# A gated mix of linear attention and a squared-ReLU layer on one Trainium2 core: the planner that lists all engines' work gets other durations and two tables of offsets, and copies may go to either of two engines

## The chip, the core and the metric

One of the eight cores of a Trainium2 chip runs the program alone. The metric is the device time of one execution in microseconds (us), the median of several. Five instruction queues run side by side and meet through semaphores: TensorE (PE, with its weight loads shown apart as PEld), VectorE (DVE), ScalarE (ACT), GpSimd (POOL) and SyncE (SP, which here only issues DMAs). Each queue takes its instructions in the order in which the program lists them.

## The reference

The input `x` is 2048 x 448. One branch is linear attention with 16 heads of 28, the other a feed-forward layer with 1792 hidden units. A sigmoid gate per row mixes them. Cut to what is computed:

```python
q, k, v = split(x @ wqkv)                      # 16 heads of 28
phi = lambda t: where(t > 0, t + 1, exp(t)) + 1e-6
kv  = einsum("bhsd,bhse->bhde", phi(k), v)     # one 28x28 matrix per head
den = einsum("bhqd,bhd->bhq", phi(q), phi(k).sum(seq)) + 1e-6
a   = (einsum("bhqd,bhde->bhqe", phi(q), kv) / den) @ wo
h   = relu(x @ w1 + b1) ** 2
b   = h @ w2 + b2
g   = sigmoid((x * gate_w).sum(-1))
out = g * a + (1 - g) * b
```

## The kernel before, in words

**Numbers as pairs.** Every float32 operand of a product is written as two parts of type float32r: a rounded "hi" copy and the rest, "lo = value - hi". A product is then three matmuls (hi hi, hi lo, lo hi). So whatever goes into TensorE first needs a copy (`split_hi`) and a subtraction (`split_lo`). `split_hi` is told its engine, mostly ACT; `split_lo` runs on DVE, for some operands on POOL.

**Two halves of the array.** A contraction of 128 rows is cut into the lower 64 rows (`LO`) and the upper 64 (`UP`). A matmul uses one half of TensorE's rows, so two matmuls run at once, one on each half; the text calls the halves lanes. All matmuls of one result accumulate in one PSUM bank, first those of one lane, then those of the other. Both lanes have the same amount to do.

**The stages.** Tokens are cut into 4 blocks of 512 and 16 tiles of 128. `h_ps{b}_{f}` is x @ w1 for block b and hidden tile f (14 of them, 21 matmuls of 512 columns each); `hidden` evicts it: ReLU on ACT, square on ACT, hi copy on DVE, lo on DVE. `o_ps{b}_{0 or 7}_{i}` is h @ w2 for 128 tokens over seven hidden tiles (matmuls of 448 columns). In the first half of the program, to about 220 us, f runs over 0 to 6 for all blocks; beside it run the keys `k_ps{t}` (450 columns), the Gram sums x'phi(k) `g_ps{b}_{c}`, then the key sums `z_ps`, `kv_ps` and `m_ps` (kv times wo). In the second half f runs over 7 to 13 for the blocks 3, 0, 1, 2, beside the queries `q_ps{b}_{c}`, the denominators `d_ps{b}`, and the attention outputs `a_ps{t}`. From a `d_ps` to the first `a_ps` of its block DVE has a long row of work: the addition of 1e-6, four reciprocals, four multiplications, and a hi and lo part for each of four tiles `q`.

**Eight PSUM banks.** Four (`acc_p`) hold `o_ps`, two (`mm_p`) `h_ps`, two (`ms_p`) everything else. A bank is used again when its last reader is done. In the first block `h_ps0_0` and `h_ps0_1` lie in `mm_p`, `h_ps0_2` and `h_ps0_3` in `ms_p`.

**What sets the order.** Nothing runs when it is written. The class `Flow` records the operations of ACT, DVE, POOL and SP (`queue`, L205), each with a cost from `cost` (L219), and the products as jobs in steps (L1000 and on). Then `run` (L375) plays the program through: again and again it asks each queue for the operation that could start first (`candidate`, L235) and each lane for the product that could start first (`product`, L329, looking `AHEAD` = 12 jobs on), takes the earliest, and writes its instruction into the program at that place. Among operations that could start at the same time the lower rank goes first; the rank is the moment when an operation was recorded plus `patience`. The constants of L32 to L35 say how long a matmul keeps its lane (`C512`, `C448`), how long after a matmul's end a reader can start (`LATE`), how long a semaphore takes (`SIGNAL`), a DMA (`LANDING`), and the change of a bank from lane to lane (`HANDED`). The numbers are only used to choose the order: on the chip each queue runs in that order and waits on semaphores.

## Time and profile before

| what | value |
|---|---|
| median of 3 runs | 440.94 us (440.69 to 441.06) |
| the profiled execution | 441.48 us, its span 439.7 us |
| granted TensorE clock | 1.000 |
| busy, of 439.7 us | PE 433.8, PEld 413.3, DVE 268.5, ACT 172.2, POOL 67.5 us |
| DMA | 29.02 MB, mean 66 GB/s |

The span runs from the first to the last instruction of the profiled execution; its own time is 1.8 us longer. A busy PE is not PE at its peak: a record of a 64-row matmul of 512 columns is 394 ns long, and two lanes with such records overlap, so that PE reads as busy when only one lane works. How fast PE goes is therefore read from how many matmuls start in a stretch.

### The profile page before, as it was taken

To read this page: it belongs to the slowest core of one execution; us is meant where nothing else is said; L and a number is where in the kernel's file an instruction comes from. 1 tells how busy PE (TensorE), PEld (TensorE's weight loads), DVE (VectorE), ACT (ScalarE), POOL (GpSimd) and SP (SyncE) were. 2 spreads that over 40 slices of the span, in tenths; PEclk is the share of its full clock that TensorE was granted. 3 is DMA by queue.
4 is the path that set the end of the run, shared out by engine and by line. 5 is a ranking of instruction groups with operands and counts; after the bars stand their busy time and mean duration, and the time that the engine had idled before them with its cause. 6 is when DMAs were issued, how large, how long until landed. Compare 5 with 4: busy or idle time off the path is not lost.

```text
span 439.7 us, 9349 instructions
## 1 busy us (share of the span) xinstructions
PE 433.8 (99%) x3978; PEld 413.3 (94%) x3978; DVE 268.5 (61%) x454; ACT 172.2 (39%) x298; POOL 67.5 (15%) x91
## 2 busy tenths in 40 slices
PE   8999999999999999999999999999999999999996
PEld 6899999999999999989999999999999899998995
DVE  4798525753587416783555849949535983458624
ACT  5846324532254214561533526415324242322530
POOL 0134104510065002530004900000000000000000
PEclk9999999999999999999999999999999999999999
DMA  7652210040111302223124631011210210001002
GB/s 255 240 152 87 76 46 25 23 138 25 41 59 45 113 3 66 83 84 92 41 86 112 110 92 49 0 64 34 62 49 1 85 25 1 0 33 55 1 1 83
DMA packets 17994, 29.02 MB, mean 66 GB/s; under 512 B 2544, under 2 KB 12448, under 8 KB 17952
## 3 DMA queue, kind: packets, MB, share of 16 engines
q1 hardware_dynamic: 16544, 26.81, 19.6%
q0 software_dynamic: 1408, 1.61, 2.2%
q8 instruction: 31, 0.51, 0.5%
q14 instruction: 11, 0.09, 0.1%
HBM read 22.08 MB, written 3.67 MB: 59 GB/s over the span
## 4 chain that ended last, share of the span: by engine, by line
PE 91%; DVE 5%; ACT 1%; DMA 1%; issue 0%; SPq 0%; DVEq 0%; ACTq 0%
PE h_ps L310 31%; PE o_ps L310 28%; PE a_ps L310 8%; PE g_ps L310 8%; PE k_ps L310 7%; PE q_ps L310 7%; DVE slot L209 4%; ACT slot L209 1%; PE kv_ps L310 1%; DMA slot<-in_xt 1%; DVE q L209 1%; PE m_ps L310 1%; PE d_ps L310 0%; ACT x L209 0%; PE z_ps L310 0%
## 5 line engine op out<-in xcount | busy, mean ns | idle before, releaser
L310 PE MATMUL h_ps<-x,w 64*128 64x512 f32 x1176 | 257.3, 394 | 0.4 <-ACT x L209 0.3
L310 PE MATMUL o_ps<-w_all,slot 64*128 64x448 f32 (+1 forms) x1332 | 240.5, 363 | 0.4 <-DVE slot L209 0.4
L310 PEld LDWEIGHTS o_ps<-w_all,slot 64*128 64x128 f32 (+1 forms) x1332 | 205.7, 184 | 6.5 <-DVE slot L209 1.8
L310 PEld LDWEIGHTS h_ps<-x,w 64*128 64x128 f32 x1176 | 193.6, 185 | 7.5 <-ACT x L209 0.8
L209 ACT ACTIVATE slot<-h_ps,few 128x512 f32<-128x512 f32 x56 | 38.0, 686 | 95.8 <-PE h_ps L310 83.8
L310 PE MATMUL q_ps<-x,wq_s 64*128 64x512 f32 x308 | 74.3, 393 | 0.0
L310 PE MATMUL k_ps<-wkm,x 64*128 64x450 f32 x336 | 66.3, 364 | 0.0
L209 DVE TENSOR_TENSOR slot<-slot,slot 128x512 fp32r<-128x512 f32 (+2 forms) x85 | 61.3, 733 | 4.4 <-DMA slot<-slot 1.7
L310 PE MATMUL a_ps<-wkm,q 64*128 64x448 f32 x336 | 62.2, 361 | 0.1
L310 PEld LDWEIGHTS k_ps<-wkm,x 64*128 64x128 f32 x336 | 57.0, 185 | 1.4 <-ACT slot L209 0.2
L310 PEld LDWEIGHTS q_ps<-x,wq_s 64*128 64x128 f32 x308 | 55.1, 184 | 1.5 <-DVE slot L209 0.3
L310 PEld LDWEIGHTS a_ps<-wkm,q 64*128 64x128 f32 x336 | 53.8, 184 | 1.3 <-DVE slot L209 0.6
L310 PE MATMUL g_ps<-p,nh 64*128 64x448 f32 x256 | 54.5, 359 | 0.0
L209 ACT ACTIVATE slot<-slot 128x512 f32<-128x512 f32 (+2 forms) x69 | 42.4, 625 | 14.7 <-DVE slot L209 13.8
L209 DVE CAST slot<-slot 128x512 fp32r<-128x512 f32 (+1 forms) x58 | 24.9, 430 | 31.9 <-ACT slot L209 30.7
L310 PEld LDWEIGHTS g_ps<-p,nh 64*128 64x128 f32 x256 | 40.6, 184 | 0.5
L209 POOL TENSOR_TENSOR nl<-slot,nh 128x384 fp32r<-128x384 f32 x16 | 19.3, 1209 | 117.6 <-ACT nh L209 117.6
L310 PE MATMUL g_ps<-p,nl 64*128 64x448 f32 x96 | 32.0, 360 | 0.0
L209 DVE SCALAR_TENSOR_TENSOR part<-part,gate,slot 128x448 f32<-128x448 f32 x13 | 8.8, 683 | 31.2 <-ACT slot L209 31.2
L209 ACT ACTIVATE slot<-a_ps,gate 128x448 f32<-128x448 f32 x16 | 10.0, 634 | 42.7 <-PE a_ps L310 40.7
L209 POOL TENSOR_TENSOR ksum<-ksum,slot 128x448 f32<-128x448 f32 x15 | 19.7, 1314 | 27.6 <-DVE slot L209 23.0
L209 DVE SCALAR_TENSOR_TENSOR slot<-slot,slot 128x448 f32<-128x448 f32 (+1 forms) x32 | 22.0, 688 | 1.7 <-ACT slot L209 1.5
(69 smaller groups left out, 350.0 us busy)
## 6 DMA issues: line engine op xcount, KB each, us to landing
slot<-in_xt SPq DMA_DIRECT2D x27, 256.0 KB, 2.8
slot<-in_xn SPq DMA_DIRECT2D x16, 224.0 KB, 2.5
out<-slot SPq DMA_DIRECT2D x16, 224.0 KB, 1.9
slot<-in_w SPq DMA_DIRECT2D x14, 224.0 KB, 2.8
slot<-in_w1a SPq DMA_DIRECT2D x8, 256.0 KB, 2.8
slot<-in_w1b SPq DMA_DIRECT2D x8, 192.0 KB, 4.0
wkm<-m POOLq DMA_DIRECT2D x24, 56.0 KB, 2.4
slot<-in_wq SPq DMA_DIRECT2D x4, 256.0 KB, 2.6
```

The costliest lines, as they stand in the source:

```text
L209: op = Op(lambda: method(*[real(x) for x in args], **{k: real(x) for k, x in kwargs.items()}), self.cost(name, kind, out, [x for x in aps ...
L310: ins = pe.matmul(b.ps[where or b.whole], real(a), real(m), start=b.seen == 1 + j.whole, stop=b.seen == b.total)
```

## The change

The reference, the products, their number and their operands stay as they are. What changes:

- **The planner's numbers.** Durations of matmuls, engine operations, signals and DMAs get other values. `cost` knows more forms (a scale per row, a read from PSUM). An engine is free again a little before an operation's end (`OVERLAP`), since the next one starts before the last is written.
- **Either engine.** A new helper `copy(to, src)` records a copy in the queues of both ACT and DVE (`either`), and the planner gives it to the engine where it would end first. `split_hi` always uses it, whatever engine its caller names; so do the copies of the first Gram sums and of `q_ps{b}_3`.
- **Two tables.** `SHIFT` adds to the rank of all operations that were recorded when a bank was done or a step entered (values from -16.5 to 33 us). `MOVE` adds to the place of a bank's job in the list of jobs (-4 to 3.5 steps), which sorts the products anew.
- **Two banks.** `h_ps0_2` and `h_ps0_3` lie in `acc_p` instead of `ms_p`.
- **Smaller things.** The key sums wait for all keys' banks in the plan, and the first tile to be done starts the sum on POOL, as the tiles now come in another order.

```diff
-C512, C448 = 0.2305, 0.204
+C512, C450, C448 = 0.2325, 0.2055, 0.2025
 AHEAD, PATIENCE, SPARE = 12, 5.0, 3
-LATE, SIGNAL, LANDING, HANDED = 0.25, 0.08, 1.9, 0.4
+LATE, SIGNAL, TO_PE, LANDING, HANDED = 0.17, 0.035, 0.09, 1.4, 0.22
+OVERLAP = {"act": 0.1, "dve": 0.085, "pool": 0.05, "sp": 0.0}
...
+SHIFT = {"a_ps0": -1.5, "a_ps1": -6, "a_ps10": 9, "a_ps11": -3, "a_ps13": -6, "a_ps14": -4.5, "a_ps15": -3, "a_ps4": 6,
...
+MOVE = {"a_ps0": 1.5, "a_ps11": 0.5, "a_ps12": 1.5, "a_ps13": 1, "a_ps14": 3.5, "a_ps15": -1.5, "a_ps2": -1.5, "a_ps3":
...
-    def __init__(self, emit, cost, after, rank, takes=None, size=0):
-        self.emit, self.cost, self.after, self.rank = emit, cost, after, rank
+
+    def __init__(self, ways, after, rank, takes=None, size=0):
+        self.ways, self.after, self.rank = ways, after, rank
         self.takes, self.size, self.end = takes, size, None
+        self.least = min((cost for _, cost in ways.values()), default=0.0)
...
+    def either(self, **calls):
+
+        self.queue({name: (getattr(unit, method), method, args, kwargs)
+                    for name, (unit, method, args, kwargs) in calls.items()})
...
-    def queue(self, name, method, kind, args, kwargs):
+    def queue(self, calls):
+        (name, (_, kind, args, kwargs)), *_ = calls.items()
         aps = [x for x in (*args, *kwargs.values()) if isinstance(x, View) or hasattr(x, "tensor")]
         out = kwargs.get("out", args[0] if args else None)
-        parts = [(x, x is out) for x in aps]
-        op = Op(lambda: method(*[real(x) for x in args], **{k: real(x) for k, x in kwargs.items()}),
-                self.cost(name, kind, out, [x for x in aps if x is not out], args),
-                {o for x, writes in parts for o in self.meeting(x, writes)}, self.now + self.patience,
+        n = next(k for k, x in enumerate(aps) if x is out)
+        ins = aps[:n] + aps[n + 1:]
+
+        def way(name, method, kind, args, kwargs):
+            return (lambda: method(*[real(x) for x in args], **{k: real(x) for k, x in kwargs.items()}),
+                    self.cost(name, kind, out, ins, args))
+        op = Op({n: way(n, *call) for n, call in calls.items()},
+                {o for x in aps for o in self.meeting(x, x is out)},
+                self.now + self.patience + SHIFT.get(self.label, 0.0),
                 out.hold if isinstance(out, View) else None, free_size(out) * list(like(out).ap)[0][1] * 4
                 if kind == "dma_start" else 0)
-        for x, writes in parts:
-            self.note(x, op, writes)
-        self.queues[name].append(op)
+        for x in aps:
+            self.note(x, op, x is out)
+        for n in calls:
+            self.queues[n].append(op)
...
+        scaled = any(free_size(x) == 1 for x in ins)
         if kind == "dma_start":
-            return 0.54 if name == "pool" else 0.06
+            return 0.51 if name == "pool" else 0.45
         if name == "act":
             f = args[2] if len(args) > 2 else None
-            return {AF.Relu: 0.26, AF.Exp: 0.18}.get(f, 0.25 if ps and f else 0.205) + n * 0.000835
+            base = 0.26 if f == AF.Relu or ps and scaled else 0.17 if ps else 0.295 if scaled else 0.2
+            return base + n * 0.000835
         if name == "pool":
-            return 0.25 + n * 0.002 if wide > 1 else 0.4 + n * 0.001
+            return 0.25 + n * 0.0021 if wide > 1 else 0.4 + n * 0.001
         if kind == "reciprocal":
-            return 0.13 + n * 0.006
+            return 0.13 + n * 0.0063
         if kind == "memset":
             return 0.1
-        return 0.155 + n / 960 if wide > 1 or ps else 0.1 + n * 0.00064
+        return 0.06 * scaled + (0.155 + n / 960 if wide > 1 or ps else 0.093 + n * 0.00064)
...
-            key = (max(start, self.free[name] + 0.05), op.rank)
+            more = op.ways[name][1] - op.least
+            key = (max(start, self.free[name] + 0.05) + more, op.rank)
             if best is None or key < best[0]:
-                best = key, start, k
-        return best and best[1:]
+                best = key, start + more, k, start
+        return best
...
-        op = self.queues[name].pop(k)
+        op = self.queues[name][k]
+        for n in op.ways:
+            self.queues[n].remove(op)
+        emit, cost = op.ways[name]
         if op.takes is not None and op.takes.buffer is None:
             place = self.vacant(op.takes.kind)[1]
             place[1], op.takes.buffer = op.takes, place[0](op.takes.dt) if callable(place[0]) else place[0]
-        self.tc.keep_in_program_order(op.emit())
-        self.free[name] = op.end = start + op.cost
+        self.tc.keep_in_program_order(emit())
+        op.end = start + cost
+        self.free[name] = op.end - OVERLAP[name]
         if op.size:
-            self.dma = max(self.dma, start + 0.6) + op.size / 385e3
+            self.dma = max(self.dma, start + 0.6) + op.size / 260e3
...
-            j.ready[s] = max([op.end + SIGNAL for op in wrote], default=0.0)
+            j.ready[s] = max([op.end + TO_PE for op in wrote], default=0.0)
...
+            self.label = b.name
             b.done()
...
-        self.jobs = [[(n, j) for n, step in enumerate(steps)
-                      for j in step.jobs[step.turn * s:] + step.jobs[:step.turn * s]] for s in range(2)]
+        self.jobs = [sorted([(n, j) for n, step in enumerate(steps)
+                             for j in step.jobs[step.turn * s:] + step.jobs[:step.turn * s]],
+                            key=lambda x: x[0] + MOVE.get(x[1].bank.name, 0.0)) for s in range(2)]
...
+    def copy(to, src):
+        flow.either(act=(nc.scalar, "activation", (to, src, AF.Copy), {}), dve=(nc.vector, "tensor_copy", (to, src), {}))
+
     def split_hi(eng, hi, src):
-        if eng is act:
-            act.activation(hi, src, AF.Copy)
-        elif eng is pool:
-            pool.tensor_scalar(hi, src, 1.0, 0.0, op0=ALU.mult, op1=ALU.add)
-        else:
-            eng.tensor_copy(hi, src)
+        copy(hi, src)
...
-        return [Job(bank, lambda: key_terms(t), C448, [("x", t // 4, False), "wk"])]
+        return [Job(bank, lambda: key_terms(t), C450, [("x", t // 4, False), "wk"])]
...
-        if t == 0:
+        if not pend:
...
-                act.copy(gsum[c], bank.ps[:, :D])
+                copy(gsum[c], bank.ps[:, :D])
...
-        return [Job(bank, key_sums, 0.07, ["zk"], [key_banks[NT - 1]])]
+        return [Job(bank, key_sums, 0.112, ["zk"], list(key_banks.values()))]
...
-        return [Job(kv_bank, kv_terms, 0.19, ["wv"], [grams[NB - 1, c] for c in range(4)])]
+        return [Job(kv_bank, kv_terms, 0.0985, ["wv"], [grams[NB - 1, c] for c in range(4)])]
...
-            act.copy(v, ps)
+            copy(v, ps)
...
-    first = [up_bank(0, f, *((mm_p, "mm") if f < 2 else (ms_p, "ms"))) for f in range(4)]
+    first = [up_bank(0, f, *((mm_p, "mm") if f < 2 else (acc_p, "acc"))) for f in range(4)]
```

In the new program ACT has 91 fewer of these copies and DVE 91 more. The program's order on each engine follows for three places. A row is one instruction, or several alike in a row (x2); in a bank's name come block, tile and half, the last number is a running one.

**TensorE, at the end of the first four `h_ps` banks.** Before, the last rows of `h_ps0_1` and what follows:

```order
L310 MATMUL h_ps0_1_210<-x0_76,w10_80 128x512
L310 MATMUL k_ps0_351<-wkm_83,x0_76 128x450 x2
L310 MATMUL k_ps0_351<-wkm_83,x1_77 128x450
L310 MATMUL k_ps0_351<-wkm_83,x0_76 128x450 x2
L310 MATMUL k_ps0_351<-wkm_83,x1_77 128x450
L310 MATMUL k_ps0_351<-wkm_83,x0_76 128x450 x2
L310 MATMUL k_ps0_351<-wkm_83,x1_77 128x450
L310 MATMUL k_ps0_351<-wkm_83,x0_76 128x450
L310 MATMUL k_ps0_351<-wkm_83,x1_77 128x450
L310 MATMUL k_ps1_376<-wkm_83,x0_76 128x450
L310 MATMUL k_ps0_351<-wkm_83,x0_76 128x450
L310 MATMUL k_ps1_376<-wkm_83,x0_76 128x450
```

After, a little later than that place (`k_ps2` has begun four rows behind the last `h_ps0_1`):

```order
L369 MATMUL k_ps0_353<-wkm_83,x1_77 128x450
L369 MATMUL k_ps2_361<-wkm_83,x0_76 128x450
L369 MATMUL o_ps0_0_0_388<-w2_all_82,slot11_365 128x448
L369 MATMUL k_ps2_361<-wkm_83,x1_77 128x450
L369 MATMUL o_ps0_0_0_388<-w2_all_82,slot11_365 128x448
L369 MATMUL k_ps2_361<-wkm_83,x1_77 128x450
L369 MATMUL o_ps0_0_0_388<-w2_all_82,slot12_375 128x448
L369 MATMUL k_ps0_353<-wkm_83,x0_76 128x450
L369 MATMUL o_ps0_0_1_400<-w2_all_82,slot11_365 128x448
L369 MATMUL k_ps0_353<-wkm_83,x0_76 128x450
```

Before, `k_ps0` stands alone over its first eleven matmuls, all in the lower lane, and the next rows of the upper lane are `k_ps0` again. Now `k_ps2` fills the upper lane beside `k_ps0`, and `o_ps0_0_0`, which reads the split `h` (slot11 is hi, slot12 lo), stands right behind them.

**VectorE, behind the denominators of block 3.** Before, the end of the row of work from `d_ps3` (which begins with two additions, four reciprocals and a read of `q_ps0_0`) up to the read that frees the bank of `q_ps0_1`, where `a_ps12` is to go:

```order
L209 TENSOR_TENSOR slot3_3660<-slot1_3849,slot3_3660 128x512
L209 TENSOR_TENSOR slot0_3739<-slot1_3849,slot0_3739 128x512
L209 TENSOR_TENSOR slot9_3583<-slot1_3849,slot9_3583 128x512
L209 TENSOR_TENSOR q2_3254<-slot8_3425,q0_3252 128x512
L209 TENSOR_TENSOR q4_3256<-slot3_3660,q1_3253 128x512
L209 TENSOR_TENSOR q6_3258<-slot0_3739,q3_3255 128x512
L209 SCALAR_TENSOR_TENSOR q7_3259<-slot9_3583,few_73,q5_3257 128x512
L209 SCALAR_TENSOR_TENSOR slot4_3857<-slot4_3857,slot10_3910 128x512
L209 TENSOR_TENSOR q5_3257<-slot9_3583,q7_3259 128x512
L209 SCALAR_TENSOR_TENSOR slot14_3842<-slot4_3857,few_73,slot14_3842 128x512
L209 CAST slot8_4004<-slot2_3890 128x512
L209 TENSOR_SCALAR slot3_4011<-q_ps0_1_3879 128x512
```

After, the same stretch; ahead of it stand two additions, four reciprocals, a hidden tile's split, four operations of block 0's `q_ps0_3`, two multiplications and the cast of q0. The bank of `q_ps0_0` takes `a_ps15`, that of `q_ps0_1` takes `a_ps13`:

```order
L258 CAST q1_3264<-slot9_3678 128x512
L258 TENSOR_TENSOR q2_3265<-slot4_3371,q0_3263 128x512
L258 TENSOR_TENSOR q3_3266<-slot9_3678,q1_3264 128x512
L258 TENSOR_TENSOR slot11_3666<-slot10_3780,slot11_3666 128x512
L258 TENSOR_TENSOR slot13_3562<-slot10_3780,slot13_3562 128x512
L258 CAST slot8_3939<-slot6_3863 128x512
L258 TENSOR_TENSOR q6_3269<-slot11_3666,q4_3267 128x512
L258 SCALAR_TENSOR_TENSOR q7_3270<-slot13_3562,few_73,q5_3268 128x512
L258 TENSOR_TENSOR slot2_3960<-slot6_3863,slot8_3939 128x512
L258 TENSOR_TENSOR q5_3268<-slot13_3562,q7_3270 128x512
L258 TENSOR_SCALAR slot9_3977<-q_ps0_0_3787 128x512
L258 TENSOR_SCALAR slot10_3986<-q_ps0_1_3900 128x512
```

The hi parts of q0 and q1 are now DVE's casts; before, all four were ACT's. From the additions to the read that frees the bank of the first `a_ps` DVE has 20 instructions before and 26 now. On TensorE 111 rows lie between the last of `d_ps3` and the first of these `a_ps` before, 142 now.

**TensorE, near the end.** Before, the first read of the split of `h_ps2_12` (slot3 is its hi part), 31 rows behind that bank's last matmul:

```order
L310 MATMUL a_ps11_5969<-wkm_83,q13_3265 128x448
L310 MATMUL a_ps11_5969<-wkm_83,q11_3263 128x448 x2
L310 MATMUL a_ps11_5969<-wkm_83,q7_3259 128x448
L310 MATMUL a_ps11_5969<-wkm_83,q2_3254 128x448
L310 MATMUL a_ps11_5969<-wkm_83,q8_3260 128x448
L310 MATMUL o_ps2_7_1_5614<-w2_all_82,slot12_5801 128x448
L310 MATMUL o_ps2_7_2_5618<-w2_all_82,slot3_5984 128x448
L310 MATMUL o_ps2_7_1_5614<-w2_all_82,slot12_5801 128x448
L310 MATMUL o_ps2_7_2_5618<-w2_all_82,slot3_5984 128x448
```

After, the first read of it (slot11):

```order
L369 MATMUL a_ps11_5966<-wkm_83,q0_3263 128x448
L369 MATMUL o_ps2_7_3_5666<-w2_all_82,slot6_5840 128x448
L369 MATMUL a_ps11_5966<-wkm_83,q10_3273 128x448
L369 MATMUL o_ps2_7_0_5639<-w2_all_82,slot11_5774 128x448
L369 MATMUL a_ps11_5966<-wkm_83,q13_3276 128x448
L369 MATMUL o_ps2_7_0_5639<-w2_all_82,slot11_5774 128x448
L369 MATMUL a_ps10_5939<-wkm_83,q9_3272 128x448
L369 MATMUL o_ps2_7_0_5639<-w2_all_82,slot12_5788 128x448
L369 MATMUL a_ps10_5939<-wkm_83,q9_3272 128x448
```

It now stands 181 rows behind the bank's last matmul: both last hidden banks, `h_ps2_12` and `h_ps2_13`, are done 150 rows and more before the program's end, and the attention tiles `a_ps8` to `a_ps11` stand behind them.

More of the change, by code (lines that the diff above doesn't have):

```diff
@@ L132, in __init__ @@
         self.tiles, self.queues, self.free, self.holds, self.kept, self.readers, self.shapes = {}, {}, {}, {}, {}, {}, {}
-        self.now, self.patience, self.dma, self.switched = 0.0, 0.0, 1.3, -1.0
+        self.label, self.now, self.patience, self.dma, self.switched = None, 0.0, 0.0, 0.0, -1.0
     def buffers(self, kind, tiles, like=None):
@@ L352, in enter @@
             if self.steps[self.entered - 1].before:
+                self.label = f"step{self.entered - 1}"
                 self.steps[self.entered - 1].before()
@@ L403, in run @@
             if event[1] == 0:
-                self.dispatch(event[3], event[4], event[0])
+                self.dispatch(*event[3:])
             else:
-                self.start(event[2], event[3], event[0])
+                self.start(event[2][0], event[3], event[0])
         if any(self.queues.values()) or any(self.at[s] < len(self.jobs[s]) for s in range(2)):
```

11 lines of the change are left out of this document (6 added, 5 removed), and 31 rows, old and new, of tables (MOVE, SHIFT).

## The prediction

> **What bounds the kernel now.** I read the page's busy times and its shares of the chain that ended last, then the groups by form for the count of matmuls, then the chain itself for TensorE's pace and for the places where it leaves TensorE.
>
> ```profile
> PE 433.8 (99%) x3978; PEld 413.3 (94%) x3978; DVE 268.5 (61%) x454; ACT 172.2 (39%) x298; POOL 67.5 (15%) x91
> PE 91%; DVE 5%; ACT 1%; DMA 1%; issue 0%; SPq 0%; DVEq 0%; ACTq 0%
> ```
>
> TensorE carries 91% of the chain, DVE 5% and ACT 1%. As no matmul is taken away, only waits can go. How much waiting is there? The counts:
>
> ```profile
> L310 PE MATMUL h_ps<-x,w 64*128 64x512 f32 x1176 | 257.3, 394 | 0.4 <-ACT x L209 0.3
> L310 PE MATMUL o_ps<-w_all,slot 64*128 64x448 f32 x1320 | 237.8, 362 | 0.4 <-DVE slot L209 0.4
> L310 PE MATMUL q_ps<-x,wq_s 64*128 64x512 f32 x308 | 74.3, 393 | 0.0
> L310 PE MATMUL k_ps<-wkm,x 64*128 64x450 f32 x336 | 66.3, 364 | 0.0
> L310 PE MATMUL a_ps<-wkm,q 64*128 64x448 f32 x336 | 62.2, 361 | 0.1
> L310 PE MATMUL g_ps<-p,nh 64*128 64x448 f32 x256 | 54.5, 359 | 0.0
> L310 PE MATMUL g_ps<-p,nl 64*128 64x448 f32 x96 | 32.0, 360 | 0.0
> ```
>
> The pace, from pieces of the chain without a wait (start, length, what), and its last pieces:
>
> ```profile
> 68.67 1.22 PE k_ps L310 x12
> 285.05 1.80 PE a_ps L310 x18
> 287.30 2.33 PE h_ps L310 x20
> ...
> 431.62 4.47 PE o_ps L310 x28
> 436.12 0.68 DVE slot L209
> ```
>
> With both lanes at work a 512-column matmul starts every 2.33/20 = 0.1165 us, one of 448 columns every 0.100, one of 450 every 0.102. So 1484 x 0.1165 + 2008 x 0.100 + 336 x 0.102 = 172.9 + 200.8 + 34.3 = 408.0 us. The small groups (`d`, `m`, `z`, `kv` and the last 12 full-height matmuls), counted in the code at these paces, I put at 11 us: 419 us of work. The first product starts at 5.38 us (row below) and the last ends at 431.62 + 4.47 = 436.09: 430.7 us. TensorE therefore loses some 12 us. A change of the order can win from these 12 alone; the 5.4 us ahead of them and the 3.6 us behind (the last bank's read, 0.68 us, and its store) stay.
>
> Where they are lost, at the start (timeline, all engines and weight loads):
>
> ```profile
> 5.38 8.85 PE L310 MATMUL h_ps<-x,w 64*128 64x512 f32 x68 [0.30 <-ACT x L209]
> 15.84 1.26 ACT L209 ACTIVATE slot<-h_ps,few 128x512 f32<-128x512 f32 x2 [1.43 <-PE h_ps L310]
> 16.58 2.37 PEld L310 LDWEIGHTS k_ps<-wkm,x 64*128 64x128 f32 x12 [0.25 <-ACT slot L209]
> 19.14 1.95 PEld L310 LDWEIGHTS k_ps<-wkm,x 64*128 64x128 f32 x20 [0.19 <-PE k_ps L310]
> 21.30 2.77 PE L310 MATMUL o_ps<-w_all,slot 64*128 64x448 f32 x25
> ```
>
> Ahead of 21.30 stand 84 `h` (4 banks of 21) and 32 `k`: 9.8 + 3.3 us, which from 5.38 would end at 18.4. So 2.9 us are lost by 21.3: 0.7 in the first 68 matmuls, whose operands are still being split, and 2.2 around `k_ps0`. There 12 loads take 2.37 us, 0.2 each: one lane alone; from 19.14 it is 0.1.
>
> Behind it 12 - 2.9 = 9.1 us are lost. What the weight loads waited for while both lanes were idle (total, times, longest), and then three of the places in the timeline:
>
> ```profile
> PEld o_ps L310 <- DVE slot L209: 1.8, 4, 0.8
> PEld d_ps L310 <- DVE slot L209: 1.0, 2, 0.5
> PEld a_ps L310 <- DVE slot L209: 0.6, 1, 0.6
> PEld h_ps L310 <- PE h_ps L310: 0.5, 1, 0.5
> PEld o_ps L310 <- DVE part L209: 0.3, 1, 0.3
> ```
>
> ```profile
> 278.02 0.18 PEld L310 LDWEIGHTS a_ps<-wkm,q 64*128 64x128 f32 x1 [0.56 <-DVE slot L209]
> 278.13 0.19 PEld L310 LDWEIGHTS a_ps<-wkm,q 64*128 64x128 f32 x1
> 278.34 0.18 PEld L310 LDWEIGHTS a_ps<-wkm,q 64*128 64x128 f32 x1
> ...
> 342.28 0.18 PEld L310 LDWEIGHTS o_ps<-w_all,slot 64*128 64x128 f32 x1 [0.81 <-DVE slot L209]
> ...
> 433.38 2.33 PEld L310 LDWEIGHTS o_ps<-w_all,slot 128*128 128x128 f32 x12 [0.31 <-DVE part L209]
> ```
>
> That is 4.2 us, 3.7 of them behind DVE. After each stop a lane loses another 0.11 us, since the first load is not hidden (the third load after 278.02 comes 0.32 later, not 0.2): for some 14 stops 1.5 us. The remaining 3.4 us are waits of one lane and intervals slightly above the pace.
>
> **Part by part.** The work that feeds TensorE:
>
> ```profile
> L209 DVE TENSOR_TENSOR slot<-slot,slot 128x512 fp32r<-128x512 f32 x60 | 45.4, 758 | 2.5 <-ACT slot L209 0.7
> L209 ACT ACTIVATE slot<-h_ps,few 128x512 f32<-128x512 f32 x56 | 38.0, 686 | 95.8 <-PE h_ps L310 83.8 <-PE o_ps L310 12.0
> L209 ACT ACTIVATE slot<-slot 128x512 f32<-128x512 f32 x60 | 37.2, 629 | 7.9 <-DVE slot L209 7.0
> L209 DVE CAST slot<-slot 128x512 fp32r<-128x512 f32 x56 | 24.6, 438 | 31.9 <-ACT slot L209 30.7 <-issue 0.8
> L209 POOL TENSOR_TENSOR nl<-slot,nh 128x384 fp32r<-128x384 f32 x16 | 19.3, 1209 | 117.6 <-ACT nh L209 117.6
> L209 DVE TENSOR_TENSOR p<-slot,p 128x448 fp32r<-128x448 f32 x16 | 17.2, 1076 | 4.6 <-ACT p L209 4.5
> ```
>
> *Copies.* 91 go from ACT (0.629 us) to DVE (0.438): DVE rises by at most 40 us to 308 of some 435, 71%, ACT falls by about 55 to 117. Nothing of that is on TensorE's path by itself; a pair of hi and lo is done 0.2 us earlier and saves a handover. Queued behind a copy on DVE are hidden tiles' splits, reads of banks, and through nh POOL's subtractions (117.6 us of waiting there, so it costs POOL nothing). The Trainium skill, page Perfetto Trace Analysis, section Optimizing Scalar/DVE Operations, says that a saturated DVE may do better with work handed to Scalar, which speaks against this step. By it the stops behind DVE would grow with its load, from 3.7 to 3.7 x 308/268 = 4.3 us, and this part would be a loss of 0.6. The rows leave it open: 71% on average is not saturated, but in one 20 us stretch it is so even now:
>
> ```profile
> 340.00:360.00 20.00, 19.62 (x175) 18.32 (x173) 19.23 (x32) 7.67 (x14) 0.00 (x0) 1.00 0.15 52
> ```
>
> *Two banks, start.* `k_ps0` no longer waits for the read of an `h` bank (0.25 us and what only one lane shows), and `k_ps2` fills the other lane. But `o_ps0_0_0` now comes right behind, and its hidden tile is late: ACT starts its ReLUs at 15.84, 0.63 apart; three ReLUs and one square end at 15.84 + 4 x 0.63 = 18.4, the cast at 18.8, a w2 cast and lo at 19.8. The lower lane has 40 of the 84 `h` and 11 of `k_ps0`: 5.38 + 0.7 + 40 x 0.233 + 11 x 0.204 = 17.6, when `o_ps0_0_0` is due. It stops 1.2 us for hi, then 0.6 for lo. The upper lane (44 `h`, ten of `k_ps2`) is queued behind it and stops for 1.5 in all. The mean with two reloads is 1.8, instead of 2.2: a gain of 0.4, between -0.5 and +1.5.
>
> *The denominators.* From the last query product to `d_ps3` lie 55 rows instead of 35, to `d_ps2` 59 instead of 41, and the hi part follows on DVE itself instead of on ACT: 20 rows are 2.2 us, more than the 1.0 us of stops. They go, with 0.2 of reloads and 0.4 of the one-lane waits, since a lane waits alone before both do: 1.6 us, at least the 1.0 of the row.
>
> *Behind the denominators.* DVE's chain into 278.02:
>
> ```profile
> 265.30 7.39 DVE slot L209 x12
> 272.69 2.47 DVE q L209 x4
> ...
> 276.37 1.61 DVE slot L209 x3
> 278.02 0.47 PE a_ps L310
> ```
>
> 20 instructions in 12.7 us, 0.64 each. The 111 rows between, at 0.109 (half 512, half 448), cover 12.1: the 0.56 lost. Now 26 instructions; at 0.60 to 0.64, as more are casts, 15.6 to 16.6 us; 142 rows cover 15.5. A stop of 0.1 to 1.1 stays; I take 0.3 and a gain of 0.5.
>
> *Near the end.* Of the last hidden tiles' splits the first read stands 150 rows and more behind their banks, 15 us, for a chain of 0.686 + 0.629 + 0.438 + 0.758 = 2.5. Before it was 31 rows, 3.1 us, hardly more than the chain with its handovers. So the 0.31 at 433.38 goes with a reload, and I place 1.0 of the one-lane waits here (0.3 to 1.5): 1.4 us.
>
> *The rest* of the 9.1: 9.1 - 1.6 - 0.8 - 1.4 = 5.3 in between. `MOVE` and the new durations spread it: from a hidden bank's close to the first read of its split lie 90 rows on average instead of 65. But the tightest are still 30 and 31 (3.0 us for 1.75 to the hi part and 2.5 to the lo part, and handovers). I take 3.8 of 5.3 as won, the o_ps and h_ps stops with their reloads (2.3 + 0.6) and 0.9 of the one-lane waits: at least 1.5, as nothing can be named in the thin spread, at most 4.8.
>
> Sum: 0.4 + 1.6 + 0.5 + 1.4 + 3.8 = 7.7 us. New stops come off it: seven hidden tiles have fewer than 40 rows, at about 0.2 us each 1.5 us (none to 3). Net 6.2. The profiled execution takes 441.48 (span 439.7), so 435.3; against the median of 440.94, 434.8. Loads move on SP with their slots, the same 116 rows; DMA is 15% busy in the stretch above, and a load that came late would cost its landing, 2.8 us at most, once.
>
> **Rivals.** *All stops go* (1 in 10): everything but 0.7 + 1.8 at the start and 1 us of spread, so 12 - 3.5 = 8.5 won: 432.4. For it speaks 90 rows on average, against it 30 and 31.
>
> *Half of it* (15 in 100): the planner's listing fits only while all durations hold; each slip is paid in an in-order queue. Then 3 us: 437.9.
>
> *No change* (6 in 100): the stops come back elsewhere; 440 to 441.8.
>
> *Slower: DVE and POOL in each other's way* (6 in 100). The p row shows a subtraction of 448 columns at 1.076 us, while one of 512 takes 0.758 on average; POOL works beside the former. That is a delay of 0.3 at least, at most a POOL instruction, 1.2; I take 0.4. About 60 of the moved copies fall into the time before 255 us in which POOL works. At 0.4 each DVE gets 24 us more there. It decides once the delay falls on hidden tiles with 30 to 37 rows, whose slack is about 0.3: at 0.8 us a stop, 8 such stops eat the gain of 6.2, and 10 make 434.8 + 8.0 = 442.8. Against it: most of these copies are loads' splits, due many us later. The Trainium skill, page SBUF — State Buffer, section Who interferes with whom, has a rule for it: DVE and GpSimd share a pair of ports under an exclusive lock, and the loser waits for the whole instruction. The p row agrees with it.
>
> **The numbers.** The forecast has 63 in 100: 434.8, its own range 433.0 to 436.7. To hold 8 in 10 the range takes in the first rival and half of the second: 432.4 to 438.3. A measurement of this kernel tells 0.2% (0.9 us) from no change. Faster 0.88, same 0.06, slower 0.06.
>
> **What would show it.** Right: DVE's and ACT's 6% of the chain fall under 3%, DVE's busy time is near 305 us and ACT's near 117, weight loads wait under 2 us in total after 21 us, `d_ps` and the last 12 loads do not wait, `o_ps0_0_0` stops near 18 us. Wrong: hidden tiles waited for between 20 and 230 us with casts of 0.8 us and more on DVE beside POOL, or `a_ps` waiting over 1 us behind the denominators.

## The result and the profile after

The changed kernel takes 444.12 us (median of 4 runs, 443.48 to 444.82) where the kernel before takes 441.0 us (440.69 to 441.16). The ratio is 1.0072, with a 95% interval from 1.0055 to 1.0089: it is slower by 0.7%, and the forecast of 434.8 us had the wrong sign. The profiled execution takes 443.48 us with a span of 441.7, at a clock of 1.0 as before. Of the runs, one of `only_act` (1101 us) and one of the kernel before (2439 us) were slow and are left out.

The page of the changed kernel, its busy times and the shares of the chain:

```profile
PE 432.3 (98%) x3978; PEld 411.1 (93%) x3978; DVE 294.6 (67%) x545; ACT 124.1 (28%) x207; POOL 65.8 (15%) x91
PE 84%; DVE 10%; issue 2%; POOL 2%; DMA 1%; ACT 1%; SPq 0%; DVEq 0%; ACTq 0%
```

DVE has its 91 instructions more and ACT its 91 less, as expected. But DVE's share of the chain went from 5% up to 10%, POOL, which was not in the list, has 2%, and TensorE's fell from 91% to 84%. The weight loads say what they waited for (total us, times, longest):

```profile
PEld o_ps L369 <- DVE slot L258: 3.5, 5, 1.7
PEld g_ps L369 <- DVE p L258: 2.8, 4, 1.2
PEld g_ps L369 <- POOL ksum L258: 1.2, 1, 1.2
...
PEld q_ps L369 <- DVE m L258: 0.6, 1, 0.6
```

The waits of `d_ps` and `a_ps` from before are gone. In their place stand waits of the hidden tiles' products, and of the Gram products `g_ps` for p, which did not wait before. Where are they? For each lane I added up how much every interval between two starts of a matmul exceeds the pace of its form, as in the prediction, and took the mean of the lanes (us; it counts what lies ahead of the first product too, 0.5 and 0.4, and every small excess, so that the sum of before is 13.4; the two kernels differ by 1.9 in this sum, and their last matmuls' starts by 2.0):

| stretch (us) | before | after |
|---|---|---|
| 0 to 22 | 3.4 | 2.3 |
| 22 to 50 | 0.3 | 4.5 |
| 50 to 140 | 1.3 | 0.6 |
| 140 to 222 | 2.0 | 3.3 |
| 222 to 240 | 0.2 | 1.9 |
| 240 to 300 | 1.7 | 1.6 |
| 300 to the end | 4.6 | 1.2 |

So from 240 us on the change won 3.5 us, and at the start 1.1. Between 22 and 240 us it lost 6.5, at four places above all: 31 to 45, 144, 201 and 222 to 232 us. Here is DVE between 20 and 60 us, first before, then after (columns: window, its length, busy us and instructions of PE, PEld, DVE, ACT, POOL, then clock, DMA share, GB/s):

```profile
20.00:40.00 20.00, 20.00 (x194) 19.52 (x192) 16.33 (x30) 11.96 (x24) 7.56 (x9) 1.00 0.37 111
40.00:60.00 20.00, 20.00 (x195) 19.74 (x193) 11.99 (x18) 7.14 (x13) 4.23 (x4) 1.00 0.22 63
```

```profile
20.00:40.00 20.00, 18.73 (x172) 16.73 (x170) 19.91 (x41) 4.01 (x8) 8.35 (x9) 1.00 0.31 89
40.00:60.00 20.00, 18.89 (x174) 17.63 (x172) 13.72 (x26) 5.34 (x9) 3.34 (x3) 1.00 0.35 111
```

After the change DVE is busy for 19.91 of the 20 us, while ACT works for 4.01. What fills DVE is seen in the timeline of the same stretch:

```profile
26.02 0.56 POOL L258 COPY ksum<-slot 128x448 f32<-128x448 f32 x1 [1.88 <-DVE slot L258]
26.41 0.41 DVE L258 CAST p<-slot 128x448 fp32r<-128x448 f32 x1
27.50 1.40 POOL L258 TENSOR_TENSOR ksum<-ksum,slot 128x448 f32<-128x448 f32 x1 [0.93 <-DVE slot L258]
27.82 1.34 DVE L258 CAST p<-slot 128x448 fp32r<-128x448 f32 x1
...
32.79 0.54 ACT L258 ACTIVATE slot<-k_ps 128x448 f32<-128x448 f32 x1 [7.60 <-PE h_ps L369]
...
33.78 0.91 PEld L369 LDWEIGHTS o_ps<-w_all,slot 64*128 64x128 f32 x9 [1.65 <-DVE slot L258]
...
36.72 1.40 POOL L258 TENSOR_TENSOR ksum<-ksum,slot 128x448 f32<-128x448 f32 x1 [0.63 <-DVE slot L258]
37.03 1.34 DVE L258 CAST p<-slot 128x448 fp32r<-128x448 f32 x1
...
44.06 0.18 PEld L369 LDWEIGHTS g_ps<-p,nh 64*128 64x128 f32 x1 [1.18 <-POOL ksum L258]
44.87 0.18 PEld L369 LDWEIGHTS g_ps<-p,nh 64*128 64x128 f32 x1 [0.62 <-DVE p L258]
```

The hi copy of p at 26.41 us starts 0.17 us before a copy on POOL ends and takes 0.41 us. The one at 27.82 starts 0.32 us behind the start of a sum of `ksum` on POOL and takes 1.34: it ends 0.26 us behind the sum, at 29.16. The copy and the sum read the same product, so 13 of the 14 copies of p on DVE overlap work of POOL. Which of the two starts first decides: seven copies that started behind POOL's instruction took 1.20 to 1.35 us, five that started 0.05 to 0.11 us ahead of the sum took 0.39 to 0.40. The row at 44.06 us names the sum, but the load there reads p, whose copy ended at 43.95, 0.25 us behind that sum. At 32.79 us ACT had been idle for 7.60 us.

The planner has a clock of its own, and it can be set beside the trace. It put the end of the last work outside SP at 435.5 us before the change, and the chip's span was 439.7. After the change it put it at 427.1, and the span was 441.7. So the planner promised 8.4 us and the chip went the other way. DVE shows where: the instruction at 20 us starts 0.8 us later than planned, the one at 33 us 3.5 us, the one at 44 us 5.6 us. The planner has 0.38 us for each of these copies; three of them, at 27.82, 37.03 and 42.62 us, last 0.95 us longer each, which is 2.9 of the 5.6 us. The rest has other sources, such as the 0.8 us from the start.

### The profile page after: what moved, and what is told of

It is laid out like the page before. It is cut to its first block, busy times and chain, and to the rows that moved or that the text cites. A ratio compares the mean times of both kernels' runs of the same rounds, so it can differ in the third digit from the quotient of the medians.

```text
span 441.7 us, 9354 instructions
## 1 busy us (share of the span) xinstructions
PE 432.3 (98%) x3978; PEld 411.1 (93%) x3978; DVE 294.6 (67%) x545; ACT 124.1 (28%) x207; POOL 65.8 (15%) x91
## 4 chain that ended last, share of the span: by engine, by line
PE 84%; DVE 10%; issue 2%; POOL 2%; DMA 1%; ACT 1%; SPq 0%; DVEq 0%; ACTq 0%
PE h_ps L369 29%; PE o_ps L369 25%; PE q_ps L369 8%; PE g_ps L369 7%; PE a_ps L369 7%; PE k_ps L369 5%; DVE slot L258 3%; DVE p L258 2%; POOL wkm L258 2%; DVE w L258 1%; DVE w_all L258 1%; PE kv_ps L369 1%; DMA slot<-in_xt 1%; ACT slot L258 1%; DVE nh L258 1%
## 5 line engine op out<-in xcount | busy, mean ns | idle before, releaser
L369 PE MATMUL h_ps<-x,w 64*128 64x512 f32 x1176 | 248.3, 394 | 0.2 <-ACT x L258 0.2
L369 PE MATMUL o_ps<-w_all,slot 64*128 64x448 f32 (+1 forms) x1332 | 230.8, 363 | 1.9 <-DVE slot L258 1.9
L369 PEld LDWEIGHTS o_ps<-w_all,slot 64*128 64x128 f32 (+1 forms) x1332 | 197.6, 184 | 7.7 <-DVE slot L258 3.5
L369 PE MATMUL q_ps<-x,wq_s 64*128 64x512 f32 x308 | 68.5, 396 | 0.1
L369 PE MATMUL g_ps<-p,nh 64*128 64x448 f32 x256 | 64.3, 363 | 2.4 <-DVE p L258 2.4
L369 PE MATMUL a_ps<-wkm,q 64*128 64x448 f32 x336 | 54.8, 360 | 0.0
L369 PEld LDWEIGHTS q_ps<-x,wq_s 64*128 64x128 f32 x308 | 50.7, 184 | 2.8 <-DVE m L258 0.6
L369 PEld LDWEIGHTS a_ps<-wkm,q 64*128 64x128 f32 x336 | 48.8, 184 | 0.5
L258 DVE CAST slot<-slot 128x512 fp32r<-128x512 f32 (+2 forms) x64 | 27.1, 426 | 27.1 <-ACT slot L258 26.3
L258 DVE TENSOR_TENSOR gsum<-g_ps,gsum 128x448 f32<-128x448 f32 x12 | 7.5, 624 | 23.3 <-PE g_ps L369 23.3
```

Source lines behind the costliest of these rows:

```text
L258: return (lambda: method(*[real(x) for x in args], **{k: real(x) for k, x in kwargs.items()}), self.cost(name, kind, out, ins, args))
L369: ins = pe.matmul(b.ps[where or b.whole], real(a), real(m), start=b.seen == 1 + j.whole, stop=b.seen == b.total)
```

## The experiments

The theories: (1) the copies stand in DVE's queue beside POOL's work, last up to 1.3 us instead of 0.4, and the planner doesn't know that; (2) the listing is too tight by its tables and shorter durations, whichever engine copies; (3) copies harm only where DVE has no idle time. Beside them, the load on DVE alone could be the cause. Most experiments keep the listing row by row and change only which engine issues some instructions. For that a line was put ahead of the one that emits an instruction, in `dispatch`. The changed kernel was not run again beside them: differences to it are between medians from different chips, on which the kernel before took 440.9 to 441.1 us, and its own four runs lie 1.3 us apart.

**copies_early_on_act.** All hi copies given to DVE from 15 to 230 us of the plan go out on ACT:

```
+        if name == "dve" and "act" in op.ways and 15.0 < start < 230.0:
+            emit = op.ways["act"][0]
         self.tc.keep_in_program_order(emit())
```

> The changed kernel with its listing kept row by row; the 99 hi copies that it gives DVE between 15 and 230 us of its plan are issued by ACT, at the same place in the program. Theory 1 (the copies fill DVE's queue, and beside POOL they last 1.3 us instead of 0.4, so that what stands behind them is late): TensorE's stops at 31 to 34, 44, 144 and 201 us go, some 5 to 6.5 us of the lane time lost there; 437.5 to 439.5 us. Theory 2 (the listing itself is too tight, by its tables and its shorter durations, whatever engine copies): 443 to 445 us, stops at the same places.

Measured: 441.02 us, ratio to before 1.0000 (0.9989 to 1.0011). That is 3.1 us faster than the changed kernel with the very same order of products. The stops at 144 and 201 us are gone, and 140 to 205 us loses 0.4 instead of 2.7; of the two waits at 44 us (1.8 us) 0.6 is left. But 0 to 50 us still loses 6.2 (6.8 in the changed kernel): now 1.9 us of waits near 18 and 20 us are behind ACT, where the first tiles' copies stand in a row, and the stop near 33 us is still 1.23 (1.65). The time lies between the two forecasts. So theory 2 falls as the main cause, and theory 1 over-estimated what the first 50 us give back.

**copies_from_20_on_act.** The same from 20 us on (`20.0 < start < 230.0`), five copies fewer.

> As the first experiment, but the five copies between 15 and 20 us of the plan stay on DVE: 94 of them are issued by ACT. In the first experiment the first hidden tile's and the weights' copies stood in one row on ACT and TensorE lost 1.2 us more ahead of 22 us. Theory 1: that comes back, the rest stays: 439.6 to 440.4 us. If the start is as long, it was the transfers' landing, which differs from run to run by some tenths: 440.8 to 441.3 us.

Measured: 439.25 us, ratio 0.9960 (0.9945 to 0.9975): 4.9 us faster than the changed kernel, faster than the kernel before, and a little better than theory 1 had it. 0 to 50 us now loses 4.6; the stop near 33 us is still 1.11. Its window has ACT at 12.32 and DVE at 16.79 of 20 us, as they were before the change:

```profile
20.00:40.00 20.00, 19.26 (x184) 18.41 (x182) 16.79 (x30) 12.32 (x24) 9.43 (x11) 1.00 0.37 115
```

**copies_late_on_act.** The 44 copies behind 230 us go to ACT (`start > 230.0`); POOL does no tensor work there.

> The same listing; the 44 hi copies on DVE behind 230 us of the plan are issued by ACT. POOL is idle there. Theory 1: these copies did no harm, and a pair of hi and lo gets 0.2 us later with another handover; 444 to 445.5 us, no stop before 240 us changes. Theory 2: the same time within 0.5 us. Should it be faster than 443.5 us, the copies harm without POOL as well, by DVE's load alone.

Measured: 444.17 us, the same as the changed kernel. Where POOL has no tensor work the copies do no harm on DVE, and no good either. Both theories allowed this time, so the run speaks only against DVE's load as the cause behind 230 us.

**pool_light.** POOL's tensor work is nearly emptied and DVE keeps all it has. The kernel leaves out POOL's subtractions and all but 8 columns of the key sums.

```
+        def thin(method, to, a, b, op):
+            if free_size(to) == D:
+                return method(real(to)[:, :8], real(a)[:, :8], real(b)[:, :8], op=op)
+            return self.nc.scalar.activation(real(to), real(a), AF.Copy)
```

> The changed kernel with its listing kept; POOL's subtractions are replaced by copies on ACT (no subtraction, no wait for the hi part) and its sums of the keys take 8 columns instead of 448, so that POOL holds nothing beside DVE. DVE's instructions are all kept. Theory 1: the copies on DVE last 0.39 us again and the stops at 33, 44, 144 and 201 us go: 437 to 439 us. If DVE's load alone makes the stops, without POOL's part in it: 442.5 to 444.5 us.

Measured: 439.11 us, ratio 0.9961 (0.9945 to 0.9977), 5.0 us faster than the changed kernel. The group of p's copies, first in the changed kernel, then here:

```profile
L258 DVE CAST p<-slot 128x448 fp32r<-128x448 f32 x14 | 12.0, 859 | 0.2
L258 DVE CAST nh<-slot 128x448 fp32r<-128x448 f32 x13 | 6.9, 532 | 0.0
```

```profile
L265 DVE CAST p<-slot 128x448 fp32r<-128x448 f32 x14 | 5.5, 394 | 0.2
L265 DVE CAST nh<-slot 128x448 fp32r<-128x448 f32 x13 | 5.0, 388 | 0.0
```

The 14 copies of p last 394 ns each instead of 859, and 22 to 50 us loses 1.3 instead of 4.5, although DVE is as full as in the changed kernel (19.64 of the 20 us from 20 to 40, with 47 instructions instead of 41). The stops at 44, 144 and 201 us are gone, but near 33 us 0.92 of 1.65 is left. So the load alone is not the cause of the whole: it makes about half of the stop near 33 us, and the others go with POOL's work, beside a DVE as full as before. The kernel also drops the waits for POOL's results; what they are worth was not taken apart.

**p_copies_on_act.** Only the 14 copies of p go to ACT (`op.takes is not None and op.takes.kind == "p"` in the place of the times).

> The changed kernel with its listing kept; only the 14 hi copies of p that it gives DVE are issued by ACT. p's sum on POOL starts with the same release as this copy. Theory 1 (the copies and POOL's work in each other's way): DVE wins up to 0.96 us at each of the ones that lasted 1.34 us, though the subtraction behind them may now meet the sum's end and last 0.3 to 0.5 us longer, as in the kernel before; some 2 of the 6 us of stops go: 441.5 to 443 us. Theory of load alone (DVE has 14 x 0.4 = 5.6 us less to do in 215 us): 443.5 to 444.3 us.

Measured: 441.73 us (441.17 to 442.33): 14 instructions of 545 make 2.4 us, half of the 4.9 and 5.0 of the two kernels above. The rows show why:

```profile
L258 DVE TENSOR_TENSOR p<-slot,p 128x448 fp32r<-128x448 f32 x16 | 12.2, 764 | 1.9 <-ACT p L258 1.9
L258 ACT ACTIVATE p<-slot 128x448 fp32r<-128x448 f32 x16 | 9.3, 579 | 23.7 <-DVE slot L258 23.7
```

DVE is rid of 12.0 us, ACT pays 14 x 0.579 = 8.1 us, for which DVE's subtractions wait 1.9 us in all, and these get no longer (764 ns, 790 in the changed kernel). The stop at 144 us goes, the waits at 44 fall from 1.8 to 1.3 and the one at 201 from 1.2 to 0.9, but near 33 us it is 1.65 as before: the copies of p alone don't make that one.

**before_p_on_dve.** The reverse, in the listing of before, which has idle time on DVE:

```
+        if name == "act" and isinstance(out, View) and out.hold.kind == "p":
+            method = lambda to, src, f: self.nc.vector.tensor_copy(to, src)
```

> The kernel before with its listing kept; only the 16 hi copies of p are issued by DVE instead of ACT, at the same place in the program. Theory 1 (the copies beside POOL's sums are the cause by themselves): as many times 0.5 to 0.96 us on DVE as in the changed kernel, and some 2 us more: 442.5 to 443.5 us. Theory 3 (the copies do harm only where DVE has no idle time left: it was busy for 16.3 of the 20 us from 20 to 40 here, 19.9 in the changed kernel): DVE's idle time takes it up, 440.7 to 441.6 us.

Measured: 443.2 us, ratio 1.0048 (1.0032 to 1.0065): 2.2 us slower, by 16 copies alone, in the old listing. Theory 3 falls: DVE's idle time does not take it up. The tables have no part in this. But the time is not lost as theory 1 had it:

```profile
L210 DVE CAST p<-slot 128x448 fp32r<-128x448 f32 x16 | 10.5, 654 | 0.3
```

Only four of the 16 copies last 1.34 us and more; eleven start 0.1 us ahead of the sum and take 0.39 to 0.40. The stops near 87 and 140 us, of 0.4 us before, grow to 1.4 and 1.5 (two waits each), and what makes them is a hidden tile's copy, here at the first of them. First the kernel before:

```profile
85.70 0.41 DVE L209 CAST slot<-slot 128x512 fp32r<-128x512 f32 x1
86.19 1.51 POOL L209 TENSOR_TENSOR nl<-slot,nh 128x384 fp32r<-128x384 f32 x1 [0.90 <-ACT nh L209]
```

Then this one:

```profile
84.64 0.56 ACT L211 ACTIVATE nh<-slot 128x448 fp32r<-128x448 f32 x1
85.28 1.21 POOL L211 TENSOR_TENSOR nl<-slot,nh 128x384 fp32r<-128x384 f32 x1
85.54 1.23 DVE L211 CAST slot<-slot 128x512 fp32r<-128x512 f32 x1
```

ACT, rid of p's copy, has nh done 0.9 us earlier, POOL's subtraction starts ahead of the hidden tile's copy instead of behind it, and that copy takes 1.23 us instead of 0.41.

**kvz_cost.** A price of the planner that has nothing to do with POOL:

```
-        return [Job(bank, key_sums, 0.112, ["zk"], list(key_banks.values()))]
+        return [Job(bank, key_sums, 0.224, ["zk"], list(key_banks.values()))]
-        return [Job(kv_bank, kv_terms, 0.0985, ["wv"], [grams[NB - 1, c] for c in range(4)])]
+        return [Job(kv_bank, kv_terms, 0.197, ["wv"], [grams[NB - 1, c] for c in range(4)])]
```

The weight loads of the changed kernel at that place show the reason:

```profile
225.97 0.67 PEld L369 LDWEIGHTS kv_ps<-gsum,slot 64*112 64x112 f32 x6
226.46 0.18 PEld L369 LDWEIGHTS q_ps<-x,wq_s 64*128 64x128 f32 x1
226.56 0.47 PEld L369 LDWEIGHTS kv_ps<-gsum,slot 64*112 64x112 f32 x4
226.85 0.18 PEld L369 LDWEIGHTS q_ps<-x,wq_s 64*128 64x128 f32 x1
```

Each product of `kv_ps` is two matmuls of 0.098 us on the chip, and the change has 0.0985 for both (0.19 before it). So the listing puts 2 or 3 products between two query matmuls, which is 4 or 6 matmuls, 0.39 or 0.59 us, where the other lane needs something every 0.232.

> The changed kernel planned with 0.197 us for a product of kv_ps (two passes of 0.098) instead of 0.0985, and 0.224 instead of 0.112 for one of z_ps. Theory: the listing gave one lane 2 or 3 kv products per query product, twice what fits, and the other lane waited 0.16 or 0.36 us at each; 1.4 us of mean lane time between 222 and 240 us come back: 442.5 to 443 us, with up to 1 us either way as the rows behind are listed anew. Rival: those waits are of the loads and come whatever the listing: 444 us.

Measured: 443.59 us (443.11 to 443.9), 0.5 faster than the changed kernel, which the spread of the runs does not tell apart. The place itself came out as expected, 222 to 240 us loses 0.4 instead of 1.9; but all behind it is listed anew, and 240 to 265 us lost 1.0 more (a wait of 1.3 us of `q_ps` for m), 300 to 350 us 0.7.

**no_tables.** `SHIFT` and `MOVE` empty, all else as changed.

> The changed kernel planned with both tables empty; durations, copies to either engine and banks as changed. By the planner's own clock the last work ends at 435.1 us instead of 427.1. Theory 1 (the tables are worth what the planner says, and the loss comes from prices that the planner has wrong): 445 to 450 us. Theory 2 (the tables make the listing too tight): 440 to 442 us.

Measured: 450.54 us, ratio 1.0208 (1.0177 to 1.0240), 6.4 us slower than with them; the planner's own clock had said 8.0, and theory 1 at most 450. From 300 us on it loses 7.3 where the changed kernel loses 1.2. The tables are worth most of what they promise, and theory 2 falls. From 22 to 50 us, though, it loses 1.6 where the changed kernel loses 4.5, so the order that the tables make has a part in the stops there.

**only_act.** Every hi copy on ACT, planned anew (`either` without its `dve` entry).

> The changed kernel planned with ACT as the only engine for every hi copy (the hidden tiles' and x's, which were DVE's before the change, among them); tables, durations and banks as changed. By the planner's own clock it ends at 430.2 us instead of 427.1. Theory 1: DVE is light before 230 us, the stops at 33, 44, 144 and 201 us go, those of kv_ps stay, and some come at the start and where a hidden tile waits for ACT: 439.5 to 442.5 us. Theory 2: 444 to 447 us, as the tables were made for another division of the work.

Measured: 444.74 us (444.18 to 444.76). That is near the time theory 2 gave. The stretch from 22 to 50 us does lose only 1.1 (4.5), near 143 us 1.7 us of waits for p stay, and the start pays the gain back, with one wait of 3.0 us as ACT now does three ReLUs, then five squares and copies, one behind the other:

```profile
17.30 2.71 ACT L258 ACTIVATE slot<-slot 128x512 f32<-128x512 f32 x5
...
19.02 0.30 PEld L369 LDWEIGHTS o_ps<-w_all,slot 64*128 64x128 f32 x4 [3.00 <-ACT slot L258]
```

**lock_tuned.** The planner gets a rule: an operation on SBUF tiles starts on DVE not before POOL's tensor operation ends, and the reverse; the `kvz_cost` prices are in it, and the tables were fitted anew by trying changes of single entries against the planner's own clock.

```
+            if op.sbuf and name in self.port:
+                a, z = self.port["pool" if name == "dve" else "dve"]
+                if a <= start < z - 0.1:
+                    start = z - 0.1
```

> The changed kernel with a planner that lets a copy, a subtraction or a product of SBUF tiles on DVE wait for the end of POOL's tensor work, and the reverse, that charges kv_ps 0.197 and z_ps 0.224 us, and whose two tables are fitted anew to that. By its own clock the last work ends at 429.2 us, 2.1 us later than the changed kernel's 427.1. Theory 1 (the planner's prices were what was wrong): the chip now follows the plan within about 2 us, the stops behind DVE between 22 and 205 us fall from 7 to under 2 us, 436 to 438.5 us, faster than both kernels. Theory 2 (a listing this tight is paid back on the chip whatever its prices): 441 us or more.

Measured: 445.37 us (443.58 in the run with a granted clock of 1.00, 445.09 to 445.89 in the three with 0.990 to 0.996), a miss. The rule did not do what the expectation says: a copy that may go to two engines is listed under ACT's name for it, and `sbuf` was set by that name, so the rule held for subtractions and products alone. The copies went on to meet POOL's sums:

```profile
31.92 1.64 DVE L228 CAST p<-slot 128x448 fp32r<-128x448 f32 x2
32.14 2.43 POOL L228 TENSOR_TENSOR ksum<-ksum,slot 128x448 f32<-128x448 f32 x2 [6.41 <-DVE slot L228]
33.48 1.34 DVE L228 CAST nh<-slot 128x448 fp32r<-128x448 f32 x1
...
44.21 0.87 PEld L346 LDWEIGHTS o_ps<-w_all,slot 64*128 64x128 f32 x5 [3.95 <-DVE slot L228]
```

DVE was 5.3 us behind its plan at 44 us, and TensorE stopped for 3.95. A fit against prices that are half right is no better than the one it replaced.

**port_tuned.** The rule mended to hold for the copies, 0.54 us for copies of 384 columns (the planner had 0.34; they last 0.54), and the tables fitted again.

```
+        op.sbuf = all(like(x).space == bass.MemoryType.SB for x in aps) and (len(calls) > 1 or kind in ("tensor_copy", "tensor_tensor", "scalar_tensor_tensor"))
...
+        if kind == "tensor_copy" and n == 384:
+            return 0.54
```

> The planner of lock_tuned did not apply its wait to the copies that go to either engine, only to subtractions and products, and had 0.34 us for copies of 384 columns that last 0.54. Both are mended here and the tables fitted anew; by its own clock the last work ends at 429.2 us (with the changed kernel's tables and these prices: 438.2 instead of 427.1). Theory 1: 435.5 to 438 us, DVE within 2 us of the plan at 45 us where the changed kernel was 5.6 us late, and faster than both kernels. Theory 2 (a listing this tight is paid back whatever its prices): 441 us or more.

Measured: 434.82 us (434.78 to 435.22), ratio to before 0.9861 (0.9846 to 0.9876): faster than both, and faster than theory 1 had it. TensorE's share of the chain is up to 97%, and from 20 to 40 us it starts 188 matmuls instead of 172, beside a DVE that is nearly as full as in the changed kernel:

```profile
PE 427.4 (99%) x3978; PEld 413.7 (96%) x3978; DVE 289.1 (67%) x539; ACT 126.7 (29%) x213; POOL 67.1 (16%) x91
PE 97%; DVE 1%; DMA 1%; ACT 0%; issue 0%; SPq 0%; ACTq 0%
```

```profile
20.00:40.00 20.00, 20.00 (x188) 19.00 (x186) 19.15 (x37) 8.16 (x17) 10.32 (x11) 1.00 0.43 120
```

DVE is 0.6 us behind its plan at 44 us. Lane time lost by stretch in the kernels that tell most (as above):

| stretch | after | from_20 | pool_light | before_p | port_tuned |
|---|---|---|---|---|---|
| 0 to 22 | 2.3 | 2.8 | 2.5 | 3.0 | 2.3 |
| 22 to 50 | 4.5 | 1.8 | 1.3 | 0.4 | 0.7 |
| 50 to 140 | 0.6 | 0.5 | 0.7 | 2.7 | 0.4 |
| 140 to 222 | 3.3 | 1.4 | 1.4 | 3.0 | 1.0 |
| 222 to 240 | 1.9 | 1.6 | 1.5 | 0.1 | 0.3 |
| 240 to 300 | 1.6 | 1.7 | 1.9 | 1.7 | 0.5 |
| 300 to the end | 1.2 | 1.3 | 1.4 | 4.2 | 1.6 |

What stays open: `port_tuned` changes the prices and the tables together, so how much of its 9.3 us against the changed kernel is the rule for DVE and POOL, how much the price of `kv_ps` and how much the new fit was not taken apart. `lock_tuned` has that price and a new fit too, without the rule for the copies, and is no faster than the changed kernel. The stop near 33 us, which neither p's copies nor POOL's work makes alone, is gone here, but no run says which of the changes did that.

## Why the prediction was wrong, point by point

- **What could be won** (12 us of lost TensorE time) holds: `port_tuned` has won 6.6 of it, close to the 6.2 of the forecast. That its 434.82 us meets the forecast's 434.8 is luck: it is another kernel than the one the forecast was made for. (440.94 - 6.2 is 434.7, not 434.8.)
- **The start**: a gain of 0.4 was forecast (-0.5 to 1.5). 0 to 22 us loses 2.3 instead of 3.4 in the profiled run, 2.5 to 2.9 in three further runs that share its first rows, as the first transfers land later or earlier: 0.5 to 1.1. `o_ps0_0_0` stopped near 18 us, as said, 0.78 and then 0.60 us.
- **The denominators and behind them**: right in mechanism. `d_ps` waits no more, and the stop of 0.56 at `a_ps` is gone wholly, where I had left 0.3. 240 to 300 us still loses as much, since `q_ps` now waits 0.6 us for m at 252.66, behind DMAs that POOL issues; I had put a late load at up to 2.8 us (the row of `in_w1b` has a median of 4.0) and didn't look for the place.
- **Near the end**: right; from 400 us on 0.4 is lost instead of 1.4, 1.0 won of the 1.4 that I put there.
- **The rest**, with the 1.5 us for new stops, is the term that failed. I took 3.8 of 5.3 us as won, less 1.5. Between 300 and 400 us 2.4 were won, and between 22 and 240 us 6.5 were lost. The step behind it: I compared the rows between a bank's close and its reader with the bare chain of the tile (2.5 us), as if the chain had DVE to itself. At 33 us DVE was 3.5 us behind the plan, and what stood in its queue stood ahead of the tile waited for at 33.78.
- **The copies**: "Nothing of that is on TensorE's path by itself" is wrong. I let DVE's mean of 71% stand for stretches in which it was at 16.33 of 20 us before anything was added; 20 to 40 us then came to 19.91. Both rows stand above. DVE's busy time itself rose by 26 us, not by the 40 that I had as the most.
- **The rival that came true** had 6 in 100: DVE and POOL in each other's way, slower, 442.8 us. Its mechanism is shown by `pool_light`, `p_copies_on_act` and `before_p_on_dve`, and the sign that I had named for it came: a hidden tile waited for at 33.78 us behind copies of 1.34 us. Its place was right only in part: in the changed kernel it is mostly the copies of p, which start with POOL's sum, and the queue behind them; the split of a tight hidden tile is hit in `before_p_on_dve`. Its price, 0.4 us a copy, was wrong: it is 0.8 to 0.97 for seven of the 13 copies of p that overlap POOL's work and next to nothing for the other six. My argument against it, that most moved copies are loads' splits due many us later, overlooked that a copy with much time of its own delays what stands behind it.
- **A price I did not question**: the diff showed `kv_ps` going from 0.19 to 0.0985. The trace of before has 64 matmuls for 32 products there; counting them would have shown the loss, which `kvz_cost` puts at 1.5 us in that stretch.
- **The Trainium skill** was weighed twice. The Trainium skill, page Perfetto Trace Analysis, section Optimizing Scalar/DVE Operations, says that offloading work of a saturated DVE to Scalar may make sense: `copies_from_20_on_act` does that and wins 4.9 us, where I had put 0.6 on it; but `port_tuned` wins twice as much with DVE at 67% of the span and 19.15 of 20 us in the same stretch, so saturation alone does not decide. The Trainium skill, page SBUF — State Buffer, section Who interferes with whom, has the loser of the port wait for the other's whole instruction; the copy that ended 0.26 us behind the sum agrees.

## What to carry to other kernels

Before believing that an order without slack is faster, check the prices behind it against a trace, contention included: a plan whose clock says 427 and whose chip says 442 has wrong prices, and the places where an engine falls behind its plan show where to look for them. Judge an engine that gets more work by its fullest stretch and by what runs beside it there, not by its mean; and when two engines share something, ask which of their instructions are released by the same event, for those meet again and again, and which of them starts first then matters.

## What the runs showed of the hardware

- Of a copy of p on DVE and POOL's work, the one that starts first goes through. In the changed kernel each copy of p that started 0.10 to 0.51 us behind a sum or subtraction on POOL ended 0.25 us behind it, and the five that started ahead took their usual 0.39. The copies of 512 columns into x that took 0.54 us instead of 0.42 fit this: they started 0.21 us behind a POOL instruction of 0.47 us and ended 0.28 to 0.29 behind it. In the kernel before 13 of the 16 subtractions of p overlap POOL's work, and each ends 0.48 or 0.49 us behind it.
- Not every copy on DVE waits. Copies of 384 columns into w took the same 0.54 us beside POOL's subtraction as alone; those at 22.66 and 29.08 us ended 0.34 and 0.41 us before it.
- The total that DVE loses beside POOL does not order the kernels. From 15 us on the instructions that overlap POOL's tensor operations exceed the shortest of their kind by about 21 us in the kernel before, 18 in the changed one, which is slower, 26 in `before_p_on_dve` and 16 in `port_tuned`. So where it falls must count besides, and whether the order leaves room there; no run here tests that by itself.
